# Moving the row-sum product of a finished attention chunk one unit earlier, directly behind the chunk's last product with V

## The chip, the cores and the metric

The kernel runs on one core of a Trainium2 chip. The metric is the device time of that core in microseconds: the median of three runs was 3857.41 us (3855.62 to 3857.58). Beside the timed runs stands one profiled execution, from which all rows in this document come. A core has engines with queues of their own: PE (matrix products; PEld is its loading of weights), DVE (vector work), ACT (activation functions and copies), POOL and SP (here mostly the issue of transfers). Each executes its own instructions in the order in which the program lists them and waits for the others through semaphores.

## The reference

The computation is four layers on a 2048 x 1024 float32 array: attention, a spectral filter, attention and the same filter again, each behind a layer norm and with a residual sum. Only the attention matters here. It has 32 heads of size 32.

```python
qkv = (x @ wqkv).reshape(B, S, 3, H, Dh)          # S = 2048, H = 32, Dh = 32
scores = einsum("bhqd,bhkd->bhqk", q, k) * Dh ** -0.5
p = softmax(scores, axis=-1)
o = einsum("bhqk,bhkd->bhqd", p, v)
out = o.reshape(B, S, D) @ wo
```

A softmax divides by the sum over all keys k. The kernel computes exp of the scores, the unnormalized product with V and the row sums separately, and divides at the end.

## The kernel before, in words

Within one attention layer the 32 heads are taken in 8 groups of 4 (`g`). For each group the 2048 queries are taken in 4 chunks of 512 (`c`), and for each chunk the 2048 keys in 16 tiles of 128 (`kt`). One (group, chunk, key tile) is called a unit, `u = 16 c + kt`; a layer has 8 x 64 units, and the program has two attention layers. Arrays are laid out with keys on the partitions and queries along the free axis.

- `S(g, c, kt)` (products on L563, exponentials on L567): 12 small products on PE (three fp16 products for each of the 4 heads, each using 32 rows of the PE array) fill two tiles of the PSUM pool `psS`; ACT then writes exp of each into two tiles `P` in SBUF, halves 0 and 1, each 128 x 1024.
- `PV(g, c, kt)` (L573): 4 heads' products of V with P, each using 32 columns of the array, accumulated over the 16 key tiles in the PSUM bank `O`. At the last key tile ACT copies `O` to `oc` (L577).
- `add(g, c, kt)` (L584, L586): DVE sums the P tiles over the key tiles into two accumulators `acc[0]` and `acc[1]`. The first key tile issues nothing, the second adds the first two (L584), the others one each (L586).
- `fin(g, c)`: four products of a constant of ones with `acc` (L592), again 32 columns each, give the row sums in a tile of `psS`; heads 0 and 1 read `acc[0]`, heads 2 and 3 `acc[1]`. DVE then works along a chain: a transpose out of PSUM (L593), a reciprocal (L595), a maximum (L596), a transpose (L598) and the division (L599). `out(g, c)` at key tile 5 of the next chunk splits the result in two fp16 halves and sends it off (L605, L606, L608).

Between these, PE is given pieces of other work, called the filler: in each odd unit a number of products for the keys, queries or values of later groups (L338, L382), or, in the last two groups, work on the output projection (L418 to L485). Their results are taken out of a PSUM pool with a single buffer (`psX`) by ACT and DVE (L167, L168), and norms of queries and keys need a small product (`norms`, L355, reduced by L357), also in a tile of `psS`.

The order on PE and on ACT is the order in which the Python code issues the instructions (`manual_schedule`). The order on DVE, POOL and SP is chosen by the framework's scheduler, which takes from the issued instructions those that its own model of the run finds ready, earlier-issued ones first. `psS` has three buffers which are taken in turn, so a tile has to wait until the tile three allocations before it has been read.

The units run two at a time. An even unit issues `S`, then `PV` of the two units before it. An odd unit issues `S`, then filler. The `add` of each unit is issued two units later. So at a chunk boundary the order on PE is: `S` of key tile 0 of the new chunk, `PV` of key tiles 14 and 15 of the old one, `S` of key tile 1, the row-sum products of `fin`, filler. There are 31 such boundaries in a layer, 62 in the program; the last chunk of each layer is finished behind the loop, by code that the change leaves alone.

Of the kernel before, what the change touches and what calls it, by code (L numbers as in the profile page):

```python
# [105 lines left out]
NG, NCH, NKT, NST = 8, 4, 16, 6  # L106
# [64 lines left out]
def run(g):  # L171
    for _ in g:
        pass
# [94 lines left out]
def attention(nc, tc, layer, ap, xin, yd, wts, wo, cst, dram, flags):  # L268
# [125 lines left out]
    def sums(ph):  # L394
        return 8 if ph[0] == "v" else 4
# [105 lines left out]
    def wo_rest(t):  # L501
        p = psS.tile([128, 2, 512], F32, name="s")
        nc.vector.bn_aggr(mvs[:, 2 * t:2 * t + 2], wo_last(t // 4, t % 4, p, wo_dst[t], wo_dst[t], True))
# [53 lines left out]
    def S(g, c, kt):  # L557

        s = [psS.tile([128, 2, 512], F32, name="s") for _ in range(2)]
        for i, (a, b) in enumerate(((0, 0), (0, 1), (1, 0))):  # L560
            for h in range(4):
                r = slice(32 * h, 32 * h + 32)
                nc.tensor.matmul(s[h // 2][:, h % 2], K[g][r, a, kt * 128:kt * 128 + 128],  # L563
                                 Q[g][r, b, c * 512:c * 512 + 512], start=i == 0, stop=i == 2)
        for hf in range(2):
            p = P[g, c, kt, hf] = pp.tile([128, 2, 512], F32, name="p")
            nc.scalar.activation(p, s[hf], AF.Exp, bias=bias[g], scale=SCALE / (SQ * SQ))  # L567

    def PV(g, c, kt):
        if kt == 0:  # L570
            O[g, c] = psO.tile([128, 512], F32, name="o")
        for h in range(4):
            nc.tensor.matmul(O[g, c][32 * h:32 * h + 32], V[g][:, kt, 32 * h:32 * h + 32], P[g, c, kt, h // 2][:, h % 2],  # L573
                             start=kt == 0, stop=kt == NKT - 1)
        if kt == NKT - 1:
            o = ap.oc.tile([128, 512], F32, name="oc")
            nc.scalar.copy(o, O[g, c])  # L577
            O[g, c] = o

    def add(g, c, kt):  # L580
        for hf in range(2):
            p = P[g, c, kt, hf]
            if kt == 1:
                nc.vector.scalar_tensor_tensor(acc[hf], P[g, c, 0, hf], 1e-34, p, op0=ALU.add, op1=ALU.add)  # L584
            elif kt:
                nc.vector.tensor_add(acc[hf], acc[hf], p)  # L586

    def fin(g, c):
        zt = on.tile([128, 16, 32], F32, name="zt")
        z = psS.tile([128, 2, 512], F32, name="s")[:, 0]  # L590
        for h in range(4):
            nc.tensor.matmul(z[32 * h:32 * h + 32], cst["ones"], acc[h // 2][:, h % 2], start=True, stop=True)  # L592
        nc.vector.transpose(zt.rearrange("p a b -> p (a b)"), z)  # L593
        rc = sm.tile([128, 16], F32, name="rc")
        nc.vector.reciprocal(rc, zt[:, :, 0])  # L595
        nc.vector.tensor_max(flags["r"], flags["r"], rc)  # L596
        r = on.tile([128, 512], F32, name="zt")
        nc.vector.transpose(r.rearrange("p (a b) -> p a b", b=32), rc.unsqueeze(2).broadcast_to([128, 16, 32]))  # L598
        nc.vector.scalar_tensor_tensor(r, O[g, c], SO, r, op0=ALU.mult, op1=ALU.mult)  # L599
        O[g, c] = r  # L600

    def out(g, c, eng=nc.vector):
        r = O.pop((g, c))
        t = on2.tile([128, 2, 512], F16, name="ohl")
        nc.scalar.copy(t[:, 0], r)  # L605
        eng.tensor_tensor(t[:, 1], r, t[:, 0], op=ALU.subtract)  # L606
        if g < NG - 1:
            nc.sync.dma_start(od[:, g, :, c * 512:(c + 1) * 512].rearrange("a p n -> p a n"), t)  # L608
        else:
            olast[c] = t  # L610

    pend, done, late = [], [], []
# [6 lines left out]
    def slots(f, sums, n, steps):  # L619

        while sums:
            k = max(1, int(n / sums + 0.5))
            m = -(-steps // k)
            for i in range(0, steps, m):
                while left_norms:
                    norms()
                for _ in range(min(m, steps - i)):
                    next(f, None)
                n -= 1
                yield sums - (i + m >= steps)  # L630
            sums -= 1

    with tc.manual_schedule(engines={mybir.EngineType.PE, mybir.EngineType.Activation}):
        for g in range(NG):
            todo = sum(sums(ph) for ph in beside.get(g, []))
            sl = slots(fill, todo, 22 if g == NG - 2 else 32, 24)
            wsl = slots(wof, 4, 10, 21)
            for u in range(NCH * NKT):
                c, kt = divmod(u, NKT)
                S(g, c, kt)  # L640
                if kt % 2 == 0:
                    for w in pend:
                        PV(*w)
                    late = pend
                    pend = []
                for w in late[:1]:
                    add(*w)
                    if w[2] == NKT - 1:
                        fin(*w[:2])
                        done = [w[:2]]  # L650
                late = late[1:]
                if kt == 5 and done:
                    out(*done.pop())
                pend.append((g, c, kt))
                if kt % 2 == 0:
                    continue
                if todo:
                    todo = next(sl)
                elif g == NG - 2:
                    if left:  # L660
                        run(lwo)
                        left = 0
                    if next(wsl, None) is not None and u == NCH * NKT - 1:
                        run(wsl)
                elif g == NG - 1:
                    for _ in range(share[u // 2]):
                        next(wof)
                    if u // 2 in rests:
                        wo_rest(rests[u // 2])
                if g == NG - 2 and todo < 4:  # L670
                    for _ in range(2):
                        if left > (8 if todo == 3 else 0):
                            next(lwo, None)
                            left -= 1
        for w in pend:
            PV(*w)
        for w in late + pend:
            add(*w)
        run(wof)
# [480 lines left out]
def build(nc, tc, a):  # L1160
    with ExitStack() as ctx:
# [29 lines left out]
        for layer in range(2):  # L1191
            y = dr.tile([2048, 1024], F32, name=f"y{layer}")
            attention(nc, tc, layer, ap, x, y, wts[layer], a["wo"], cst, dr, flags)
            x = a["out"] if layer else x1
            if layer:
                spectral(nc, tc, ap, y, x, a, cst, True)
            else:
                spectral(nc, tc, ap, y, x, a, cst, True, flags, (s for ph in PH0 for s in wts[1].prep(ph)))
# [40 lines left out]
```

## Time and profile before

| what | value |
|---|---|
| median of the timed runs | 3857.41 us |
| the profiled execution, its own time | 3855.25 us |
| span of its profile (first to last instruction) | 3853.3 us |
| PE busy | 97% of the span |
| DVE busy | 82% |
| ACT busy | 75% |
| mean granted TensorE clock | 0.99 |

In the profile's rows a group of instructions stands as line, engine, operation, what it writes and reads, shape and count, then busy time, mean duration and the idle time of the engine just before. In the timeline each row begins with the start and the length in microseconds, counted from the start of the span; neighbouring instructions of the same kind are merged (`x12`), and brackets tell how long the engine had been idle before and what ended that. Matmul lengths include the pipeline's tail, so starts are the safer thing to compare. One row-sum "product" is two matmul instructions in float32, so a `fin` shows as 8 matmuls and a pair of `PV` as 16.

### The profile page before, as it was taken

The numbers are of one execution on the slowest core, as the hardware profiler recorded it, in microseconds if no ns is written. First come the engines' busy times: TensorE is split into PE (matmuls) and PEld (weight loads), VectorE is DVE, ScalarE is ACT, GpSimd is POOL, SyncE is SP. The second block draws the span as 40 slices with busy tenths as digits, with TensorE's granted clock in tenths as the row PEclk, the third lists the DMA queues.
The fourth block names the chain that finished last, engine by engine and source line by source line (L and its number), as shares of the span: only waits on it lengthen the run. The fifth ranks groups of instructions, "written<-read, shape, count | busy, mean of one in ns | idle before, by whom it ended". The sixth has DMA issues, their size and how long they took to land.

```text
span 3853.3 us, 79584 instructions
## 1 busy us (share of the span) xinstructions
PE 3720.5 (97%) x32951; PEld 1640.1 (43%) x32951; DVE 3165.8 (82%) x3869; ACT 2898.3 (75%) x3567; POOL 303.0 (8%) x386
## 2 busy tenths in 40 slices
PE   6999999999999999999989999999999999999998
PEld 4322433342234233378853334333423432333788
DVE  6699899889998988866666998899899889889554
ACT  4678887888788866667756888888888888666585
POOL 1000000000000000004320000000000000000143
PEclk9999999999999999999999999999999999999999
DMA  8000000000000221243270000000000002112433
GB/s 206 15 12 23 12 12 18 18 12 18 12 26 7 73 71 64 80 149 124 63 175 15 18 18 13 12 18 23 10 18 12 23 12 91 53 64 72 150 99 104
DMA packets 165573, 194.07 MB, mean 50 GB/s; under 512 B 74960, under 2 KB 120656, under 8 KB 164176
## 3 DMA queue, kind: packets, MB, share of 16 engines
q1 hardware_dynamic: 164912, 188.82, 15.9%
q8 instruction: 260, 4.26, 0.5%
q14 instruction: 113, 0.93, 0.1%
q10 hardware_dynamic: 288, 0.07, 0.0%
HBM read 123.83 MB, written 48.23 MB: 45 GB/s over the span
## 4 chain that ended last, share of the span: by engine, by line
PE 73%; DVE 12%; issue 8%; ACT 3%; DMA 2%; POOL 2%; SPq 0%; DVEq 0%; POOLq 0%; ACTq 0%
PE o L573 19%; PE s L563 16%; PE x L338 12%; PE x L382 7%; PE x L441 6%; DVE R L586 4%; PE s L441 2%; PE ps L861 2%; PE ps L801 2%; ACT p L567 1%; PE s L592 1%; PE ps L792 1%; DMA wst<-in_wp 1%; PE ps L976 1%; PE ps L930 1%
## 5 line engine op out<-in xcount | busy, mean ns | idle before, releaser
L567 ACT ACTIVATE p<-s,bias 128x1024 f32<-128x1024 f32 x2048 | 2167.8, 1111 | 553.5 <-PE s L563 542.6
L586 DVE TENSOR_TENSOR R<-R,p 128x1024 f32<-128x1024 f32 x1792 | 2085.4, 1219 | 111.2 <-ACT p L567 107.8
L573 PE MATMUL o<-p,R 128*32 128x512 f32 x8192 | 985.0, 598 | 0.0
L338 PE MATMUL x<-big,wqk 128*128 128x512 f16 x2880 | 682.7, 383 | 21.1 <-DVE Q L168 6.5
L563 PEld LDWEIGHTS <-R 32*128 32x128 f16 x12288 | 231.6, 92 | 760.3 <-issue 644.6
L338 PEld LDWEIGHTS <-wqk 128*128 128x128 f16 x3072 | 277.6, 98 | 458.5 <-issue 165.4
L563 PE MATMUL s<-R 32*128 32x512 f16 x6144 | 430.9, 378 | 10.6 <-ACT p L567 8.9
L573 PEld LDWEIGHTS o<-p,R 128*32 128x32 f32 x8192 | 213.7, 109 | 523.8 <-issue 523.8
L563 PE MATMUL s<-Q,R 32*128 32x512 f16 x6144 | 425.4, 378 | 7.5 <-DVE R L482 5.5
L382 PEld LDWEIGHTS <-big 128*128 128x128 f16 x3072 | 293.1, 99 | 144.3 <-issue 66.2
L382 PE MATMUL x<-wv,big 128*128 128x256 f16 x2688 | 320.5, 275 | 35.0 <-DMA big<-hl 35.0
L584 DVE SCALAR_TENSOR_TENSOR R<-p 128x1024 f32<-128x1024 f32 x128 | 153.8, 1203 | 198.9 <-ACT p L567 198.6
L441 PE MATMUL x<-big 128*128 128x512 f16 x1050 | 241.6, 380 | 0.0
L363 POOL PARTITION_ALL_REDUCE mall<-mqk x16 | 41.8, 2612 | 2325.5 <-DVE mqk L357 2313.9
L441 PEld LDWEIGHTS <-big 128*128 128x128 f16 x1344 | 124.3, 98 | 180.5 <-issue 42.7
L909 DVE TENSOR_TENSOR H<-G,H 128x512 f16<-128x512 f32 (+1 forms) x68 | 46.3, 680 | 113.1 <-ACT H L908 112.9
L861 PE MATMUL ps<-cbi,H 128*128 128x256 f16 (+1 forms) x792 | 100.5, 275 | 7.9 <-ACT H L908 6.2
L854 ACT COPY U<-ps 64x256 f32<-64x256 f32 (+1 forms) x272 | 97.0, 357 | 11.6 <-PE ps L861 6.4
L854 ACT COPY B<-ps 64x256 f32<-64x256 f32 (+1 forms) x272 | 97.0, 356 | 7.0 <-PE ps L861 2.8
L861 PE MATMUL ps<-cb,big 128*128 128x256 f16 x780 | 97.6, 275 | 0.0
L167 ACT ACTIVATE R<-x 128x512 f16<-128x512 f32 x88 | 52.6, 598 | 54.8 <-PE x L338 54.7
L806 DVE TENSOR_TENSOR big<-ps,big 128x512 f16<-128x512 f32 x64 | 44.4, 694 | 50.4 <-ACT big L805 50.3
(428 smaller groups left out, 2967.7 us busy)
## 6 DMA issues: line engine op xcount, KB each, us to landing
wst<-in_wp SPq DMA_DIRECT2D x96, 256.0 KB, 3.0
R<-y SPq DMA_DIRECT2D x32, 512.0 KB, 5.4
w<-in_w SPq DMA_DIRECT2D x60, 256.0 KB, 2.7
od<-ohl SPq DMA_DIRECT2D x56, 256.0 KB, 2.4
big<-od SPq DMA_DIRECT2D x16, 896.0 KB, 7.0
y<-R SPq DMA_DIRECT2D x20, 512.0 KB, 2.6
R<-in_x SPq DMA_DIRECT2D x16, 512.0 KB, 5.6
wst<-in_wo SPq DMA_DIRECT2D x32, 256.0 KB, 3.0
```

The lines of the kernel that those rows point to most:

```text
L167: nc.scalar.activation(hi, src, AF.Copy, scale=scale)
L338: nc.tensor.matmul(ps, a, b, start=d == 0 and i == 0, stop=d == 7 and i == 2)
L382: nc.tensor.matmul(ps[:, j], l, r, start=d == 0 and i == 0, stop=d == 7 and i == 2)
L441: nc.tensor.matmul(p, a, b, start=start and d == ds[0] and i == 0, stop=stop and d == ds[-1] and i == 2)
L563: nc.tensor.matmul(s[h // 2][:, h % 2], K[g][r, a, kt * 128:kt * 128 + 128], Q[g][r, b, c * 512:c * 512 + 512], start=i == 0, stop=i == 2)
L567: nc.scalar.activation(p, s[hf], AF.Exp, bias=bias[g], scale=SCALE / (SQ * SQ))
L573: nc.tensor.matmul(O[g, c][32 * h:32 * h + 32], V[g][:, kt, 32 * h:32 * h + 32], P[g, c, kt, h // 2][:, h % 2], start=kt == 0, stop=kt == ...
L584: nc.vector.scalar_tensor_tensor(acc[hf], P[g, c, 0, hf], 1e-34, p, op0=ALU.add, op1=ALU.add)
L586: nc.vector.tensor_add(acc[hf], acc[hf], p)
L801: nc.tensor.matmul(pa[:, j], tt[:, j], mm[:, g], start=True, stop=True)
L854: nc.scalar.copy(ov[64 * r:64 * r + 64, a0:a0 + m, x], tl[64 * x:64 * x + 64, :m, r])
L861: nc.tensor.matmul(out, l, r, start=k == 0, stop=k == len(mm_) - 1)
```

## The change

The call of `fin` moves from unit 1 of a chunk to unit 0. There the two outstanding `add`s, of key tiles 14 and 15, are both issued at once, and the row-sum products follow directly behind `PV` of the key tiles 14 and 15; `S` of key tile 1 now comes behind them. `out` still runs at key tile 5. On PE the order at a boundary becomes: `S` of key tile 0, `PV` of 14 and 15, the row-sum products, `S` of key tile 1, filler. The tile of `psS` that takes the row sums is now allocated before the two of key tile 1. No instruction is added or removed.

```diff
@@ -643,11 +643,14 @@
                         PV(*w)
                     late = pend
                     pend = []
+                    if kt == 0 and late:
+                        for w in late:
+                            add(*w)
+                        done = [late[1][:2]]
+                        fin(*done[0])
+                        late = []
                 for w in late[:1]:
                     add(*w)
-                    if w[2] == NKT - 1:
-                        fin(*w[:2])
-                        done = [w[:2]]
                 late = late[1:]
                 if kt == 5 and done:
                     out(*done.pop())
```

## The prediction

> **What bounds the kernel now.** I read the page first: busy shares, then the chain that ended last.
>
> ```profile
> PE 3720.5 (97%) x32951; PEld 1640.1 (43%) x32951; DVE 3165.8 (82%) x3869; ACT 2898.3 (75%) x3567; POOL 303.0 (8%) x386
> ...
> PE 73%; DVE 12%; issue 8%; ACT 3%; DMA 2%; POOL 2%; SPq 0%; DVEq 0%; POOLq 0%; ACTq 0%
> PE o L573 19%; PE s L563 16%; PE x L338 12%; PE x L382 7%; PE x L441 6%; DVE R L586 4%; PE s L441 2%; PE ps L861 2%; PE ps L801 2%; ACT p L567 1%; PE s L592 1%; PE ps L792 1%; DMA wst<-in_wp 1%; PE ps L976 1%; PE ps L930 1%
> ```
>
> PE is the bound: 97% busy and 73% of the chain. What the change is worth is what it adds to or takes from PE's time at the 62 boundaries, plus any wait of PE elsewhere that grows or shrinks because DVE or ACT is shifted. Second, the row-sum line and what it waits for:
>
> ```profile
> L592 PE MATMUL s<-R,ones x512: 589/593/617, 172.9 to 3550.6; 128*32 128x512 f32 x171
> L592 PEldq EVENT_SEMAPHORE  x62: 51/51/51, 172.2 to 3546.2; - x62
> ...
>   DVE R L586: 5.3, 8
> ```
>
> 512 matmuls are 64 row sums of 8; 62 of them are moved. Today they wait for DVE's sums only 5.3 us in all. Third, the timeline of one boundary (group 0 of the second layer):
>
> ```profile
> 2272.19 3.49 DVE L586 TENSOR_TENSOR R<-R,p 128x1024 f32<-128x1024 f32 x3
> ...
> 2273.09 0.83 PE L563 MATMUL s<-Q,R 32*128 32x512 f16 x12
> ...
> 2273.84 1.92 PE L573 MATMUL o<-p,R 128*32 128x512 f32 x16
> 2273.95 2.12 ACT L567 ACTIVATE p<-s,bias 128x1024 f32<-128x1024 f32 x2 [0.47 <-PE s L563]
> 2274.30 0.13 PEld L573 LDWEIGHTS o<-p,R 128*32 128x32 f32 x4 [0.30 <-issue]
> ...
> 2275.70 0.83 PE L563 MATMUL s<-Q,R 32*128 32x512 f16 x12
> ...
> 2276.46 1.06 PE L592 MATMUL s<-R,ones 128*32 128x512 f32 x8
> 2276.56 2.12 ACT L567 ACTIVATE p<-s,bias 128x1024 f32<-128x1024 f32 x2
> ...
> 2277.46 1.90 PE L338 MATMUL x<-big,wqk 128*128 128x512 f16 x8
> 2277.71 1.23 DVE L584 SCALAR_TENSOR_TENSOR R<-p 128x1024 f32<-128x1024 f32 x1 [2.04 <-ACT p L567]
> 2278.85 0.71 DVE L593 STREAM_TRANSPOSE zt<-s 128x512 f32<-128x512 f32 x1
> ...
> 2279.29 0.83 PE L563 MATMUL s<-Q,R 32*128 32x512 f16 x12
> ```
>
> From start to start PE spends 0.76 us on a block S, 1.86 on the 16 matmuls of PV and 1.00 on the 8 of the row sum. PV and row sum have the same form (128 rows x 32 columns, f32), so 8 matmuls cost 1.86 - 1.00 = 0.86, and each block pays 1.00 - 0.86 = 0.14 once, when PE changes to a block of another form.
>
> **The change, part by part.**
>
> *One change of form less.* Now the forms alternate S, PV, S, row sum, filler; after the change PV and row sum are one run. The row sum starts 1.86 - 0.14 = 1.72 after PV's start, and the boundary is 0.14 shorter. From above: all 0.14. From below: nothing, if the cost belongs to each block and not to the form. The nearest row is PV itself: it holds two key tiles with different weights and operands, and no second 0.14 shows in it (two halves of 0.86 and one 0.14). I take 0.14. The Trainium skill, TensorEngine Tiling (Array Packing), Key Properties, says that changing the tiling mode drains the engine; by that rule too the term is the whole 0.14 and not nothing.
>
> *The row sum waits earlier.* It needs the sums of key tile 15, and is now asked for 2.62 - 1.72 = 0.90 us sooner. Where DVE is done by then nothing is paid:
>
> ```profile
> 2363.64 2.36 DVE L586 TENSOR_TENSOR R<-R,p 128x1024 f32<-128x1024 f32 x2 [0.25 <-ACT p L567]
> ...
> 2365.00 1.93 PE L573 MATMUL o<-p,R 128*32 128x512 f32 x16
> ```
>
> Here the sums end at 2366.00 and the new place is 2365.00 + 1.72 = 2366.72. I found 46 boundaries of this kind, the tightest in the last group but one (sums end at 3219.08, new place 3219.52):
>
> ```profile
> 3215.59 3.49 DVE L586 TENSOR_TENSOR R<-R,p 128x1024 f32<-128x1024 f32 x3
> ...
> 3217.80 1.92 PE L573 MATMUL o<-p,R 128*32 128x512 f32 x16
> ```
>
> Eight are like 2273: first chunk of a group, sums end at 2275.68, the new place is 2275.56; with 0.06 for the signal (below) the second half waits 0.18, net +0.04. Six are late already: the first chunk of groups 0 to 5 of the first layer, where a maximum over loaded weights (L259) stands ahead of the last sums. The first and the last of them:
>
> ```profile
> 170.96 2.35 DVE L586 TENSOR_TENSOR R<-R,p 128x1024 f32<-128x1024 f32 x2
> ...
> 172.90 1.51 PE L592 MATMUL s<-R,ones 128*32 128x512 f32 x8
> ...
> 1082.77 1.32 DVE L259 TENSOR_REDUCE fw<-wst 128x1 f32<-128x512 f32 x2
> 1084.00 2.35 DVE L586 TENSOR_TENSOR R<-R,p 128x1024 f32<-128x1024 f32 x2
> ...
> 1085.68 1.77 PE L592 MATMUL s<-R,ones 128*32 128x512 f32 x8
> ```
>
> The row sum is busy for 1.51 and 1.77 instead of 1.06, because its second half waits for the sum. It will end at the same moment, and the S that stood before it, its cover, now stands behind: +0.76 each. The last two boundaries (group 7, second chunk) wait for a PSUM buffer that DVE frees at 1525.78; now S waits for it, then the row sum would, with the same end. Nothing.
>
> ```profile
> 1525.83 0.83 PE L563 MATMUL s<-Q,R 32*128 32x512 f16 x12 [1.44 <-DVE R L482]
> ```
>
> *S of key tile 1 comes later.* It starts 2.72 after PV instead of 1.86, so its exponentials do too, by 0.86. That is hidden: ACT's exponentials for key tile 0 end at 2276.07, before S needs their buffer (2276.56), and ACT then waits at each boundary for filler anyway. Without that cover it would cost up to 0.86 x 62.
>
> *The row-sum tile is taken before those of key tile 1*, so S of key tile 2, 5.31 after PV's start, must now wait for the transpose L593 (today S of key tile 3 does). The row sum ends 1.72 + 1.06 = 2.78 after PV's start; with 0.06 and 0.71 the transpose is done at 3.55. Free, with 1.76 to spare, if DVE executes it at once.
>
> *DVE's idle time at the boundary is filled.*
>
> ```profile
> L584 DVE SCALAR_TENSOR_TENSOR R<-p 128x1024 f32<-128x1024 f32 x128 | 153.8, 1203 | 198.9 <-ACT p L567 198.6 <-PE s L592 0.3
> L338 PE MATMUL x<-big,wqk 128*128 128x512 f16 x2880 | 682.7, 383 | 21.1 <-DVE Q L168 6.5 <-DVE R L168 6.2 <-ACT wqk L167 5.4
> L563 PE MATMUL s<-R 32*128 32x512 f16 x6144 | 430.9, 378 | 10.6 <-ACT p L567 8.9 <-DVE mqk L357 1.6
> L355 PE MATMUL s<-sq,bones 128*32 128x512 bf16 x128 | 15.4, 387 | 9.4 <-DVE sq L342 6.9 <-ACT p L567 1.6 <-POOL sq L342 1.0
> ```
>
> Some 199 us, about 3 a boundary, DVE idles before L584 for the exponentials. Now the row sum's chain can start at 2276.85 in the boundary above (second half at 2275.74, 1.06 long, 0.05), where DVE sat until 2277.71. The chain's four operations last about 1.8 and end at 2278.7, when L584 can start too (S of key tile 1 at 2276.74, then 0.86 and 1.15 as in the rows). So DVE is 0.8 ahead. This matters where DVE stays busy up to a wait of PE:
>
> ```profile
> 2298.93 0.42 DVE L342 TENSOR_TENSOR sq<-R 128x512 bf16<-128x512 f16 x1
> ...
> 2298.28 0.40 PE L355 MATMUL s<-sq,bones 128*32 128x512 bf16 x3
> 2299.41 0.38 PE L355 MATMUL s<-sq,bones 128*32 128x512 bf16 x1 [0.73 <-DVE sq L342]
> ...
> 2120.99 0.39 PE L563 MATMUL s<-R 32*128 32x512 f16 x2
> 2121.62 0.82 PE L563 MATMUL s<-R 32*128 32x512 f16 x10 [0.24 <-DVE mqk L357]
> ...
> 242.59 1.67 PE L338 MATMUL x<-big,wqk 128*128 128x512 f16 x7 [2.48 <-DVE Q L168]
> ```
>
> (L342 ends at 2299.35, PE goes on at 2299.41: the 0.06 used above.) The norm's wait of over 1 us at 2299 stands in three groups of the second layer: 3 x 0.8. The 0.6 at 2121 stands four times: 4 x 0.6. The one at 242 stands three times in the first layer (even groups); there DVE's lead less PE's own 0.14 counts: 3 x 0.7. Sum 6.9. From above, all of DVE's share in these three rows, 6.5 + 1.6 + 6.9 = 15; from below 0, since DVE's order is the scheduler's and I don't know it. I take 6.9.
>
> *Sum:* -46 x 0.14 + 8 x 0.04 + 6 x 0.76 - 6.9 = -6.4 + 0.3 + 4.6 - 6.9 = -8.4 us. Against the profiled execution (3855.25 us, span 3853.3) that is 3846.9; the median shown is 2.2 us higher, so 3849.0.
>
> **Rivals.** *A: the transpose stands behind L584 on DVE, as it does now (2277.71, then 2278.85).* Then S of key tile 2 waits on it: L584 can start 4.9 after PV's start (2278.75), L593 1.14 later, done at 6.75, with the signal 6.8, against 5.31. That is 1.5 us a boundary with 8 filler matmuls, less with longer filler: at most 62 x 1.5 = 93, I say 65: 3920 us, slower. It decides once L593 ends later than 5.25. For it: today's order. Against: today both become ready together (S and row sum are neighbours on PE); afterwards the row sum is 1.9 us earlier.
>
> *B: the row sum pays its own start.* No 0.14 is saved; the eight then cost 0.18 and the six 0.90, +6.8 in all, and DVE's 6.9 cancel it: 3857 us, no change. Against it: PV's two key tiles without a gap. The Trainium skill, TensorE: Matmul & The Clock Gate, Part 3, The mechanism, says that weight loads overlap running matmuls only if their row groups differ; here all 128 rows are the same, so the row sum's first load (0.108 by the row below) would lie open and the first term shrink to 46 x 0.03, the sum to about -3. The trace disagrees: the PV loads at 2274.30 (0.13 us) lie inside the PV block, in the same rows.
>
> ```profile
> L592 PEld LDWEIGHTS s<-R,ones 128*32 128x32 f32 x512 | 10.9, 108 | 32.5 <-ACT p L567 24.6 <-DVE R L586 3.9 <-ACT oc L577 2.4
> ```
>
> *C: DVE's lead brings nothing*, since the scheduler puts other work there. Then -1.5: 3856 us.
>
> **How the numbers follow.** About 0.2% (7.7 us) is what a measurement can tell from none. Forecast 0.60 (its own range 3844 to 3853, two thirds of it beyond 0.2%), A 0.08, B 0.10, C 0.17, another order on DVE 0.05. So faster 0.43 (0.40 and 0.03 of the rest), same 0.44 (a third of the forecast, 0.09 of B, 0.15 of C), slower 0.13 (A, and what is left of the others). The range 3842 to 3862 leaves out A and takes in DVE's upper bound in part and B without DVE's gain (+6.8).
>
> **What would show it.** Row sum 1.72 after PV's start, S 1.00 after it, filler 0.76 after that; at the six late boundaries the wait for L586 grows, past today's 5.3 us in the L592 view; L593 before L584 on DVE and the 199 us idle much smaller; smaller shares for L342, L357 and Q L168. I am wrong if S of key tile 2 waits for L593, if the row sum starts at 1.86, or if other sums run late because DVE's order changed.

## The result and the profile after

| kernel | median of the timed runs | profiled span |
|---|---|---|
| before | 3856.46 us (20 runs) | 3853.3 us |
| changed | 3849.91 us (20 runs, 3842.39 to 3853.98) | 3845.7 us |

The ratio is 0.9982, with a 95% interval of 0.9975 to 0.9988: faster by 6.6 us, about 0.2%. The forecast was 3849.0 us. All medians and ratios here are of executions at a granted clock of 0.99; one later execution of the changed kernel and one of the mixed kernel below were granted 0.85 and 0.83, took 4246.83 and 4309.14 us, and are left out. The busy shares and the chain that ended last, of the changed kernel:

```profile
PE 3713.8 (97%) x32951; PEld 1644.1 (43%) x32951; DVE 3184.0 (83%) x3869; ACT 2897.4 (75%) x3567; POOL 309.1 (8%) x386
...
PE 79%; DVE 9%; issue 5%; DMA 3%; ACT 2%; POOL 2%; SPq 0%; DVEq 0%; POOLq 0%; ACTq 0%
```

PE is still the bound, and now holds 79% of the chain instead of 73%. DVE's part has gone from 12% to 9%, although DVE is busy a little longer (3184.0 us against 3165.8). The boundary that answers to the one at 2273 in the prediction, in the timeline of the changed kernel (counted from the first `S` of the layer it lies in group 1 of the second layer, not in group 0 as the prediction says):

```profile
2274.64 1.92 PE L573 MATMUL o<-p,R 128*32 128x512 f32 x16
...
2276.38 1.19 PE L592 MATMUL s<-R,ones 128*32 128x512 f32 x8
2277.51 0.83 PE L563 MATMUL s<-Q,R 32*128 32x512 f16 x12
2277.62 0.72 DVE L593 STREAM_TRANSPOSE zt<-s 128x512 f32<-128x512 f32 x1 [1.16 <-PE s L592]
2278.27 1.90 PE L338 MATMUL x<-big,wqk 128*128 128x512 f16 x8
...
2278.38 0.25 DVE L595 RECIPROCAL rc<-zt 128x16 f32<-128x16 f32 x1
...
2279.56 0.69 DVE L599 SCALAR_TENSOR_TENSOR zt<-oc,zt 128x512 f32<-128x512 f32 x1
2280.10 0.83 PE L563 MATMUL s<-Q,R 32*128 32x512 f16 x12
2280.17 2.35 DVE L584 SCALAR_TENSOR_TENSOR R<-p 128x1024 f32<-128x1024 f32 x2
```

The row sum starts 1.74 us after PV. Its length of 1.19 instead of 1.04 (below) is the short wait of its second half for DVE's sums. From PV to the filler it is 3.63 us, and 3.62 before: this boundary costs nothing and gains nothing. On DVE the transpose (L593) and the whole chain behind it now run ahead of both L584. Before, DVE executed one L584 first. A boundary where DVE is in time, in the second layer, in the same kernel:

```profile
2411.48 1.92 PE L573 MATMUL o<-p,R 128*32 128x512 f32 x16
2413.22 1.04 PE L592 MATMUL s<-R,ones 128*32 128x512 f32 x8
2414.20 0.83 PE L563 MATMUL s<-R 32*128 32x512 f16 x12
2414.95 1.90 PE L338 MATMUL x<-big,wqk 128*128 128x512 f16 x8
```

From PV to the filler it takes 3.47 us. The same boundary before took 3.61:

```profile
2411.29 1.92 PE L573 MATMUL o<-p,R 128*32 128x512 f32 x16
2413.15 0.83 PE L563 MATMUL s<-R 32*128 32x512 f16 x12
2413.90 1.07 PE L592 MATMUL s<-R,ones 128*32 128x512 f32 x8
2414.90 1.90 PE L338 MATMUL x<-big,wqk 128*128 128x512 f16 x8
```

From the view of the row sum's line in the changed kernel, how long and how often it waits for DVE's sums, and then the groups of two operations on DVE (busy time, mean ns, idle time ahead of them and what ended it):

```profile
  DVE R L586: 9.5, 12
```

```profile
L584 DVE SCALAR_TENSOR_TENSOR R<-p 128x1024 f32<-128x1024 f32 x128 | 150.7, 1217 | 36.9 <-ACT p L567 36.9
L593 DVE STREAM_TRANSPOSE zt<-s 128x512 f32<-128x512 f32 x64 | 45.8, 715 | 111.4 <-PE s L592 111.4
```

The wait for L586 grew from 5.3 to 9.5 us. DVE's idle time ahead of L584 fell from 198.9 to 36.9 us, but ahead of L593, where it had been 0.0, stand 111.4. Together DVE idles some 51 us less at the boundaries, about 0.8 us at each.

To see where the time went, I cut each trace at the start of `S` of key tile 0, so that a piece is one chunk of one group (the last of the second layer ends at its last block `S`, and the last of the first layer reaches to the first `S` of the second), and took the difference of each piece to the same piece in the first profile of before. The table gives sums over the pieces of a class, each the mean of three profiled executions (least and most in brackets). "Order of before" are the two profiles of before and that of the experiment with the sums issued early, whose order on PE is that of before. "Mixed" are the three profiles of the two kernels in which the six late boundaries keep the order of before (their experiments are below).

| boundaries in the pieces | number | order of before | changed | mixed |
|---|---|---|---|---|
| DVE in time, nothing else near | 27 | -0.01 (-0.02 to 0.00) | -3.74 (-3.75 to -3.73) | -3.75 |
| with a norm behind the boundary (start of groups 1, 3, 5) | 6 | 0.00 | 0.50 (0.49 to 0.51) | 0.50, 0.50 and 0.00 |
| first chunk of a group finished, DVE barely late | 8 | -0.01 | -2.60 (-2.63 to -2.55) | -2.62 |
| the six late ones of the first layer | 6 | 0.77 (-0.98 to 3.30) | 6.07 (5.88 to 6.17) | 0.13 |
| third chunk of groups 0, 2, 4, 6, first layer | 4 | 0.31 (-0.74 to 1.68) | -2.99 (-3.34 to -2.65) | -2.96 |
| third chunk of groups 0, 2, 4, second layer | 3 | 0.00 | -0.73 | -0.73 |
| third chunk of group 7, both layers | 2 | 0.00 | 0.00 | 0.00 |
| third chunk of group 6, second layer | 1 | -1.88 (-3.21 to 0.00) | -3.68 (-3.85 to -3.57) | -3.76 |
| all others (first and last pieces of the layers, fourth chunks of groups 0, 2 and 4 of the first layer) | 7 | 0.0 | -1.6 | -0.9 |
| sum | 64 | -0.8 | -8.8 | -14.3 |

The order of the change stands 8.0 us below that of before, near the 6.6 that the medians give. Where the brackets are wide, the pieces differ between executions of the same kernel or order by up to 4 us, and a mean of three is rough; the last two rows ahead of the sum are of this kind.

### The profile page after: what moved, and what is told of

Same layout as the page of the kernel before. It is cut to its first block, busy times and chain, and to the rows that moved or that the text cites. A ratio compares the mean times of both kernels' runs of the same rounds, so it can differ in the third digit from the quotient of the medians.

```text
span 3845.7 us, 79600 instructions
## 1 busy us (share of the span) xinstructions
PE 3713.8 (97%) x32951; PEld 1644.1 (43%) x32951; DVE 3184.0 (83%) x3869; ACT 2897.4 (75%) x3567; POOL 309.1 (8%) x386
## 4 chain that ended last, share of the span: by engine, by line
PE 79%; DVE 9%; issue 5%; DMA 3%; ACT 2%; POOL 2%; SPq 0%; DVEq 0%; POOLq 0%; ACTq 0%
PE o L573 22%; PE s L563 18%; PE x L338 14%; PE x L382 7%; PE x L441 6%; DVE R L586 2%; PE s L441 2%; PE ps L864 2%; PE s L592 2%; PE ps L804 1%; PE ps L795 1%; DMA wst<-in_wp 1%; DMA w<-in_w 1%; PE ps L979 1%; ACT p L567 1%
## 5 line engine op out<-in xcount | busy, mean ns | idle before, releaser
L586 DVE TENSOR_TENSOR R<-R,p 128x1024 f32<-128x1024 f32 x1792 | 2087.3, 1217 | 128.3 <-ACT p L567 124.9
L584 DVE SCALAR_TENSOR_TENSOR R<-p 128x1024 f32<-128x1024 f32 x128 | 150.7, 1217 | 36.9 <-ACT p L567 36.9
L593 DVE STREAM_TRANSPOSE zt<-s 128x512 f32<-128x512 f32 x64 | 45.8, 715 | 111.4 <-PE s L592 111.4
L857 ACT COPY U<-ps 64x256 f32<-64x256 f32 (+1 forms) x272 | 97.2, 357 | 10.9 <-PE ps L864 5.7
L864 PEld LDWEIGHTS <-H 128*128 128x128 f16 (+1 forms) x792 | 76.7, 99 | 20.6 <-ACT H L911 7.5
```

Source lines behind the costliest of these rows:

```text
L857: nc.scalar.copy(ov[64 * r:64 * r + 64, a0:a0 + m, x], tl[64 * x:64 * x + 64, :m, r])
L864: nc.tensor.matmul(out, l, r, start=k == 0, stop=k == len(mm_) - 1)
```

## The experiments

The theory was that of the prediction: the gain is one change of form less on PE and an earlier DVE, and the six late boundaries take most of it back, because `S` no longer covers their wait. The rivals: that the adds, issued a unit earlier, do it alone; that the row sum's place behind a block of its own form is worth nothing; and that the place of the transpose on DVE, not PE's order, decides.

**The sums issued early, the row sum left where it was.** Both `add`s are issued in unit 0, `fin` in unit 1.

```diff
                     if kt == 0 and late:
                         for w in late:
                             add(*w)
                         done = [late[1][:2]]
-                        fin(*done[0])
                         late = []
+                if kt == 1 and done:
+                    fin(*done[0])
```

> One part alone: both adds of the finished chunk are issued in unit 0, the row sum stays in unit 1 behind S of key tile 1. My theory (the gain is one change of form less on PE at each boundary, and the place of the row-sum chain on DVE) expects no change against the kernel before: ratio 1.000, within 0.1%, and L584 ahead of L593 on DVE as before. The rival that the gain comes from the earlier issue of the adds expects 0.998, like the changed kernel.

Measured 3854.29 us against 3853.87 of before, ratio 0.9998 (0.9989 to 1.0007). The groups on DVE look like those of before:

```profile
L584 DVE SCALAR_TENSOR_TENSOR R<-p 128x1024 f32<-128x1024 f32 x128 | 153.8, 1203 | 199.7 <-ACT p L567 198.4 <-PE s L592 1.3
L593 DVE STREAM_TRANSPOSE zt<-s 128x512 f32<-128x512 f32 x64 | 45.4, 709 | 0.0
```

So the earlier issue of the sums does nothing. DVE's new order comes from the row sum's new place on PE.

**The change without the six late boundaries.** There the old order stays; everywhere else the new one.

```diff
-                    if kt == 0 and late:
+                    if kt == 0 and late and (layer or g > 5 or c != 1):
...
                 for w in late[:1]:
                     add(*w)
+                    if w[2] == NKT - 1:
+                        fin(*w[:2])
+                        done = [w[:2]]
```

> The changed kernel, except that the six boundaries where DVE's sums are late (first chunk of groups 0 to 5 of the first layer) keep the old order. My theory: those six chunks grew by 1.00, 1.12, 0.69, 1.09, 0.91 and 1.36 us, 6.2 in all, because S of key tile 1 no longer covers the wait; kept as before they cost nothing: some 6 us less than the changed kernel, ratio to before near 0.9967. The rival that the first layer's loss comes from another order on DVE brought about by the change expects 0.998, as the changed kernel.

Measured 3842.97 us, ratio 0.9973 (0.9964 to 0.9983). One late boundary (group 3 of the first layer) shows what is kept. In the timeline of before:

```profile
717.39 1.92 PE L573 MATMUL o<-p,R 128*32 128x512 f32 x16
719.24 0.83 PE L563 MATMUL s<-Q,R 32*128 32x512 f16 x12
720.96 2.09 PE L592 MATMUL s<-R,ones 128*32 128x512 f32 x8 [0.89 <-DVE R L586]
722.99 1.90 PE L338 MATMUL x<-big,wqk 128*128 128x512 f16 x8
```

In that of the changed kernel:

```profile
719.60 1.92 PE L573 MATMUL o<-p,R 128*32 128x512 f32 x16
723.21 2.10 PE L592 MATMUL s<-R,ones 128*32 128x512 f32 x8 [1.68 <-DVE R L586]
725.24 0.83 PE L563 MATMUL s<-Q,R 32*128 32x512 f16 x12
726.00 1.90 PE L338 MATMUL x<-big,wqk 128*128 128x512 f16 x8
```

From PV to the filler 5.60 us became 6.40, and nearly all of that is the 0.76 of `S`, which now stands behind the wait instead of inside it. This boundary alone varies between executions (5.14 us in the second profile of before, 5.55 in that of the changed kernel), so all six are better: their stretches from PV to the filler sum to 31.8 us with the change and to 27.2 in the mixed kernels, each the mean of three profiles. That is 4.5 less, or 0.75 each. In the table the six pieces cost 6.07 with the change and 0.13 without.

**A tiny product of the same form ahead of the row sum.** Its result is overwritten; nothing is left out.

```diff
+        nc.tensor.matmul(z[0:32, 0:32], cst["ones"], cst["ones"], start=True, stop=True)
         for h in range(4):
```

> The changed kernel with one tiny product of constants (ones by ones, 128 rows x 32 columns, 32 wide) put between PV and the row sum, 64 times; its result is overwritten. It has the form of its neighbours. Both theories expect only its own time, some 0.03 to 0.1 us each: 2 to 6 us over the changed kernel, ratio to before 0.9987 to 0.9998. It is the control for e_form.

Measured 3847.37 us, ratio 0.9981 (0.9972 to 0.9990). It costs 0.04 us a boundary in the pieces (27 of them stand at -0.10 instead of -0.14).

**A tiny product of another form in the same place.** It uses all 128 columns of the array.

```diff
+        nc.tensor.matmul(z[:, 0:32], cst["ident"], cst["ones"], start=True, stop=True)
         for h in range(4):
```

> As e_same, but the tiny product has another form (identity by ones, 128 rows x 128 columns), so that PE changes form twice between PV and the row sum. If a change of form costs 0.14 us, each boundary pays the 0.14 that the change had saved and about as much again: 62 x 0.24 to 0.28, 15 to 17 us over e_same, ratio to before near 1.003. If the cost belongs to each block and not to the form (rival B), e_form and e_same take the same time within 2 us.

Measured 3874.43 us, ratio 1.0052 (1.0038 to 1.0065): 27 us more than with the same form, where 15 to 17 were expected, and 0.43 more in each of the 27 plain pieces. The timeline of this kernel, with the loads of weights (PEld):

```profile
2429.36 1.92 PE L573 MATMUL o<-p,R 128*32 128x512 f32 x16
...
2431.22 0.30 PEld L591 LDWEIGHTS s<-ones,ident 128*128 128x128 f32 x2 [0.84 <-issue]
2431.22 0.41 PE L591 MATMUL s<-ones,ident 128*128 128x32 f32 x2
...
2431.56 1.06 PE L593 MATMUL s<-R,ones 128*32 128x512 f32 x8
```

And that of the kernel with the same form:

```profile
2410.19 1.92 PE L573 MATMUL o<-p,R 128*32 128x512 f32 x16
...
2411.50 0.11 PEld L591 LDWEIGHTS s<-ones 128*32 128x32 f32 x1 [0.30 <-issue]
2411.93 0.19 PE L591 MATMUL s<-ones 128*32 128x32 f32 x1
...
```

The other form starts 1.86 us after PV, exactly as `S` did before; the same form starts 1.74 after. With the same form the first load runs 0.43 us ahead of its product, inside PV; with the other form the loading stands idle for 0.84 us and starts together with the product. So the price belongs to the change of form, and it shows as a load that isn't hidden. The Trainium skill, TensorEngine Tiling (Array Packing), Key Properties, says that a switch of the tiling mode drains the engine. These rows agree and give the size: 0.12 us on the way in. The two changes of form explain some 0.28 of the 0.43. The rest, about 0.15, I put to the tiny product's own load of 128 columns (0.30 for its two loads), but no run measured that part alone.

**The transpose forced behind the first L584.** PE's order is that of the change; on DVE the first half of `add` of key tile 1 comes first, then the chain, then the second half. The main part of the edit:

```diff
+                if kt == 1 and done:
+                    with tc.issue_after(add(g, c, 1, (0,)).ins):
+                        chain(*done[0], *zs)
+                    add(g, c, 1, (1,))
```

> The changed kernel with DVE's old order forced at the boundary: the first L584 of the new chunk, then the transpose out of PSUM (here L597), as the trace of before has it; PE's order is that of the changed kernel. My rival A prices it: S of key tile 2 waits for the transpose, 1.5 us at a boundary with 8 filler matmuls, less with longer filler, together 65 us over the changed kernel, ratio to before near 1.015. If the order on DVE does not matter the ratio stays at 0.998. If only DVE's lead is lost and PE does not wait for the transpose, the mid-chunk gains go and the ratio is 0.9995.

Measured 3901.93 us, ratio 1.0125 (1.0109 to 1.0140); the change beside it gave 0.9980, so this order of DVE costs about 55 us. The price is near the expectation, the mechanism is not. In the timeline of this kernel:

```profile
2452.37 0.83 PE L563 MATMUL s<-R 32*128 32x512 f16 x12
...
2453.23 2.12 ACT L567 ACTIVATE p<-s,bias 128x1024 f32<-128x1024 f32 x2 [0.83 <-PE s L563]
2454.38 1.22 DVE L584 SCALAR_TENSOR_TENSOR R<-p 128x1024 f32<-128x1024 f32 x1 [4.59 <-ACT p L567]
...
2454.96 1.26 PE L563 MATMUL s<-R 32*128 32x512 f16 x12
2455.41 0.32 PEld L563 LDWEIGHTS <-R 32*128 32x128 f16 x9 [0.35 <-issue]
2455.52 0.71 DVE L597 STREAM_TRANSPOSE zt<-s 128x512 f32<-128x512 f32 x1
...
2456.16 1.06 PE L573 MATMUL o<-p,R 128*32 128x512 f32 x8
```

`S` of key tile 2 starts 2.59 us after the one before it, as in the changed kernel (2277.51 and 2280.10), and does not wait for the transpose, which starts only at 2455.52. It is stretched to 1.26 instead: its loads go on at 2455.41, when ACT's exponentials of key tile 1 end (2453.23 + 2.12 = 2455.35). So it took a buffer that key tile 1 had used, and not that of the row sums. The buffers of `psS` are not simply taken in turn, as the description ahead of the prediction has it; what decides which one is taken, no run shows. This costs 0.44 at this place (PV 1.20 after `S` instead of 0.76). By the pieces of the table, against the changed kernel, this order costs 9.0 us at the 27 plain ones, 4.6 at the six with a norm, 10.7 at the eight, 11.2 at the six late ones, 10.2 at the four third chunks of the first layer, and the rest elsewhere. Which waits stand behind these sums, beside the 0.44 shown, I did not work out.

**The changed kernel and before once more**, to see what repeats.

> The changed kernel once more, for a second profile: chunks with a clean boundary 0.14 us shorter than before, the six late ones longer by 0.7 to 1.4, as in the first. The 3.6 us that the third chunk of group 6 of the second layer gained in the first profile stand beside a wait for a transfer; if that is a difference between executions and not of the change, it is not the same here. Ratio 0.998.

> The kernel before once more, for a second profile: chunk by chunk the same times within 0.1 us, except where PE waits for transfers (the third chunk of group 6 in each layer, the stretches between the attention loops), which shows how much of a difference between two profiles is not of the change.

The changed kernel gave 3846.84 us beside the last experiment, ratio 0.9980 (0.9971 to 0.9989); before, one execution, 3855.02. In the second layer every piece of before repeated to 0.02 us except two: the third chunk of group 6 took 50.39 us instead of 53.61, and the piece that opens the layer 0.61 less. In the changed kernel's first profile that chunk took 50.03. So most of that row of the table is not the change's doing. In the first layer the same chunk took 50.39 and 50.40 in the two profiles of before and 49.75 to 49.76 in the three of the changed kernel.

**The six late boundaries and the norm boundaries left in the old order.** The pieces had shown +0.08 at each start of an odd group with a norm, where -0.14 was expected. One more condition beside that of the mixed kernel:

```diff
-                    if kt == 0 and late and (layer or g > 5 or c != 1):
+                    if kt == 0 and late and (layer or g > 5 or c != 1) and (c or g not in (1, 3, 5)):
```

Its times stand beside those of the mixed kernel and of the changed one.

> As e_mixed, and the six boundaries that a norm's product follows (start of groups 1, 3 and 5 of both layers) keep the old order too: there the chunk grew by 0.08 us instead of losing 0.14. Expected by the chunk times: 6 x 0.08 = 0.5 us below e_mixed, which only the profile can show (those chunks 0.00 against before instead of +0.08); ratio to before 0.997.

> e_mixed once more, on the same chip as the changed kernel beside it, to tell whether it beats it. My theory: 6 us below the changed kernel, ratio to before near 0.9967. The rival (the six late boundaries cost nothing in the end): the same as the changed kernel, 0.998.

> The changed kernel beside e_mixed and e_best on the same chip: ratio to before 0.998, 6 us above e_mixed by my theory.

| kernel | median | ratio to before |
|---|---|---|
| changed | 3848.38 us | 0.9983 (0.9975 to 0.9992) |
| mixed | 3842.03 us | 0.9967 (0.9956 to 0.9978) |
| mixed, norm boundaries too in the old order | 3842.36 us | 0.9970 (0.9958 to 0.9982) |

Side by side the mixed kernel is 6.4 us below the changed one, as expected, and it beats both kernels of this case. (Its first experiment, with 3842.97 beside 3853.87 of before, had it 10.9 us below before, where the change had brought 6.6.) The norm boundaries went back to 0.00 in the pieces, all six, but 0.5 us cannot be told apart in the times.

## Why the prediction came out right

The time and the case held likeliest were right: faster by about 0.2%, by the mechanism named, though the sizes of its terms were less exact than the time. Term by term:

| step of the prediction | predicted | measured |
|---|---|---|
| one change of form less, 46 boundaries | -6.4 | -0.139 each at the 27 plain ones; six others +0.08 |
| eight boundaries barely late | +0.3 | +0.1: 0.01 at the one quoted (3.63 against 3.62) |
| six late boundaries | +4.6 | +5.3 against the order of before, +5.9 against the mixed kernels, for the whole pieces |
| DVE's lead | -6.9 | -5.7 |

The lead is worked out from the table: the eight without their own 0.01 each (-2.60 - 0.08 = -2.7), the three of the second layer without the form's 0.14 each (-0.73 + 0.42 = -0.3) and the four of the first layer against the mean of before, again without 0.14 each (-2.99 - 0.31 + 0.56 = -2.7).

*The change of form* was exact: 0.14 from PV to the filler, and 3.74/27 = 0.139 in the pieces. The rival by which the row sum pays its own start is out: the row sum starts 1.74 after PV, not 1.86, and the two tiny products show that only another form pays.

*Six late boundaries.* The mechanism was right (`S` no longer covers the wait), and so was the size at the boundary itself: 0.75 each against the mixed kernels, where 0.76 was predicted. What the prediction left out comes later in the same chunks, about 1.4 us in all by the same comparison. A part of it stands in groups 1, 3 and 5, where DVE is late for the norm of the same chunk too: from starts in the first profiles of both kernels, PE waited 1.62, 1.84 and 1.69 us there before and 2.03, 2.14 and 2.26 after, 1.3 more in all. Over three profiles each it is 1.2 more than in the order of before, but only 0.6 more than in the mixed kernels. That DVE passes its delay on fits this; no run shows it alone, and the rest is open.

*DVE's lead.* The sign and the order on DVE were right (L593 ahead of L584); so the rival in which the lead brings nothing is out, and the one in which the transpose stands behind L584 did not happen. But a lead of 0.8 was carried through to the later waits, and more than half of it is lost on DVE itself. At the wait that the prediction quotes at 2299, in the timeline of the changed kernel:

```profile
2299.09 0.40 PE L355 MATMUL s<-sq,bones 128*32 128x512 bf16 x3
2299.41 0.41 DVE L342 TENSOR_TENSOR sq<-R 128x512 bf16<-128x512 f16 x1
2299.88 0.38 PE L355 MATMUL s<-sq,bones 128*32 128x512 bf16 x1 [0.39 <-DVE sq L342]
```

The wait shrank from 0.73 to 0.39. Counted from PV, L342 starts at 24.77 instead of 25.09, a lead of 0.32. The idle time saved was 2.04 - 1.16 = 0.88. The rest went between the instructions. The nine operations of DVE from the boundary to the next sums stand interleaved in the timeline of before (first L584, transpose, second L584, and then the rest of the chain between other work):

```profile
2279.49 1.18 DVE L584 SCALAR_TENSOR_TENSOR R<-p 128x1024 f32<-128x1024 f32 x1
...
2282.30 0.69 DVE L599 SCALAR_TENSOR_TENSOR zt<-oc,zt 128x512 f32<-128x512 f32 x1
2282.90 4.63 DVE L586 TENSOR_TENSOR R<-R,p 128x1024 f32<-128x1024 f32 x4
```

They take from 2277.71 to 2282.90, 5.19 us. In the changed kernel the same nine, with the chain in one run, take from 2277.62 to the next sum:

```profile
2283.04 0.41 DVE L342 TENSOR_TENSOR sq<-R 128x512 bf16<-128x512 f16 x1
2283.38 1.22 DVE L586 TENSOR_TENSOR R<-R,p 128x1024 f32<-128x1024 f32 x1
```

That is 5.76, 0.57 longer, and 0.88 - 0.57 is the lead of 0.31. Nearly every operation of the chain needs the one just before it (the second transpose needs the reciprocal, two before it): the reciprocal starts 0.04 after the end of the transpose (2277.62 + 0.72 = 2278.34, then 2278.38), where independent neighbours start before the end of the one ahead (the transpose at 2278.85 lasts 0.71, and L584 starts at 2279.49). The Trainium skill, VectorE: DVE Perf Modes, The DRAIN you can't avoid, says that the next operation starts only when the pipe is empty, and earlier where it isn't held. The rows show both kinds of start; that a dependence is what delays the later ones is my reading of them. So the eight boundaries of the kind at 2273 brought 2.7, or 0.34 each, where 4.8 (3 x 0.8 + 4 x 0.6) had been counted for seven of them. The first layer's third chunks brought 2.7 instead of 2.1, but this is rough, since the same four pieces lie between -0.74 and 1.68 in the order of before. Another 0.3 came from three chunks that were not counted.

*Norm boundaries, missed.* The prediction put these six with the plain ones. There `norms` takes a tile of `psS` right behind `S`. In the timeline of before DVE reduces it (L357) ahead of most of the chain, and `S` of key tile 2 has its usual length:

```profile
2236.24 0.65 DVE L357 TENSOR_REDUCE mqk<-s 128x1 f32<-128x512 f32 x1
2236.65 0.83 PE L563 MATMUL s<-Q,R 32*128 32x512 f16 x12
```

In the changed kernel it comes only behind the whole chain:

```profile
2236.11 0.69 DVE L599 SCALAR_TENSOR_TENSOR zt<-oc,zt 128x512 f32<-128x512 f32 x1
2236.72 0.68 DVE L357 TENSOR_REDUCE mqk<-s 128x1 f32<-128x512 f32 x1
2237.10 1.17 PE L563 MATMUL s<-Q,R 32*128 32x512 f16 x12
```

`S` of key tile 2 is stretched to 1.17 us, because its second half waits for L357, which ends at 2237.40. This was named as a way to be wrong, but for L593, and not for the norm's tile behind it. The stretch of 0.34 (1.17 for 0.83) outweighs the 0.26 that these boundaries gain from PV to the norm's product (3.62 for 3.88). Against the -0.14 expected it costs 0.22 each, 1.3 in all.

*The sum.* With the measured sizes it is -6.4 + 1.3 + 0.1 + 5.3 - 5.7 = -5.4 instead of -8.4: the late boundaries and the missed norms took 2.0 more, the lead gave 1.2 less, the eight cost 0.2 less. The measured 6.6 lies between the two, and the interval of the ratio (0.9975 to 0.9988 of 3856.46, or -9.6 to -4.6) holds both. The last two rows of the table, which vary between executions, stand 3.4 us lower with the change, 2.6 without the 0.14 of their own six boundaries. These 2.6 are what separates the -5.4 from the -8.0 of the table, and whether any of them is the change's doing stays open. That the forecast of 3849.0 came within 0.9 us of the median is in part luck: its terms were 3.0 too hopeful together, the median of before came out 0.95 lower over twenty runs than in the three shown (3856.46 for 3857.41), and some of the gain measured belongs to no term of the sum.

*The rival on the slower side* was wrongly built, though of the right size: the transpose behind L584 would cost about 55 us, but not by a wait of `S` for the transpose. The step under it, that `S` of key tile 2 must wait for L593 because the buffers are taken in turn, is not borne out where it was put to the test. In the changed kernel it makes no difference, since the transpose ends at 2278.34 and `S` starts at 2280.10.

## What to carry to other kernels

Where the bounding engine alternates between blocks of different tile forms, putting two blocks of one form next to each other saves a fixed price per change; count the changes and read the price from a block's length with and without its neighbour. A block that waits for another engine wants independent work ahead of it on its own queue, so move it forward only where its operand is there in time: here the move at 56 of 62 boundaries was worth 10.9 and 14.1 us in its two experiments, and the move at all of them 6.6 to 8.8 in three. And when an engine's idle time is filled by a chain of dependent operations, count the gaps between these as well: part of the gain stays there.

## What the runs showed of the hardware that had not been expected

- On PE the price of a change of form shows in the loads: within one form the next load of weights starts some 0.43 us ahead of its product, inside the running block; across a change it starts together with the product (2431.22 in the kernel with another form). One tiny product of another form costs 0.48 us at a plain boundary of the changed kernel, and one of the same form 0.04.
- On DVE the same nine operations took 5.19 us interleaved and 5.76 with the dependent ones in a run.
- One chunk (third of group 6, second layer) took 53.61 us in one profiled execution of before and 50.39 in another, while its neighbours agreed to 0.02 us. A single pair of profiles would have given the change 3 us too much.
